# Projection products with 512 columns in one instruction instead of two halves of 256

## The chip, the cores and the metric

The kernel runs on one core of a Trainium2 chip, alone. The metric is the device time of one execution in microseconds (us); the lower the better. Five engines of the core work beside each other, each through its own list of instructions: TensorE (PE in the profile, its weight loads apart as PEld), VectorE (DVE), ScalarE (ACT), GpSimd (POOL) and SyncE (SP), which here issues the transfers.

## The reference, cut to what matters

Attention in chunks of 64 tokens is followed by two feed-forward layers over the 4,608 tokens; all arrays are float32.

```python
scores = scale * np.matmul(q_c, k_c.transpose(0, 1, 2, 4, 3))      # 8 x 8 heads, 9 chunks of 64, depth 64
attn = np.exp(scores - np.max(scores, axis=-1, keepdims=True))
attn = attn / (np.sum(attn, axis=-1, keepdims=True) + 1e-09)
out = np.matmul(attn, v_c)
...
h = np.maximum(np.maximum(x @ w1, x @ w2), x @ w3)                 # (4608, 512) @ (512, 768), three times
x = h @ w_out                                                      # (4608, 768) @ (768, 512)
...
h = np.maximum(x @ w_in, 0.0)                                      # (4608, 512) @ (512, 2048)
return (h * h @ w_out).astype(np.float32)                          # (4608, 2048) @ (2048, 512)
```

## The kernel before

Tokens are worked on in 9 blocks of 512 (`b`). Every float32 operand of a large product is kept as a sum of two float32r tiles, a high and a low part (names that end in h and l), and a product is made of three: high by high, high by low, low by high.

**The first half of the program** (to about 704 us) does the attention and the first feed-forward layer. `proj` is one projection product: for a slice `f` of 128 of the 768 columns and one of the three weights `w` (0 to 2), it adds 4 depth slices by 3 pairs into one bank `p` of PSUM (128 x 512). There are 9 x 6 x 3 = 162 of them, and two `p` banks that alternate. What comes out is taken by ScalarE for w = 0 (line 383) and by VectorE for w = 1 and 2 (lines 386 and 390), so product n + 2 can begin when product n has been taken. `g2` is the first output product: for each of the 6 slices `f` it adds 3 pairs into each of 4 `y` banks; there are 54 x 4 such groups. Both go through `mm_k` and `halves`, line 355. Before the change `halves` gives each pair as two instructions of 256 columns (HC = 256), which follow each other with the same weights. Three of the projection products at the very start are made in two parts of 256 columns each (`parts=2`), so that `dst` has only 256 columns there and `halves` has nothing to cut.

The blocks 2 to 8 run the loop `for f: for w: p1(b, f, w)`, with one step of the attention (scores S, transposes T, outputs X) after w = 0 as long as there is attention to do, and the output product of the slice before after w = 1. In the last block there is no attention left. In the first 125 us the input arrives, weights are split by ScalarE, VectorE and GpSimd, and a hand-made order of attention and products runs. A few bfloat16 products of zeros (`heat`, line 568, 512 columns each) stand in gaps there.

**The second half** (the products `z` of line 449 and `o` of line 500) uses Strassen's seven products on 256-column operands. The change doesn't touch it.

The weights of w = 1 lie in tiles of `shifted`, whose parts begin 64 bytes (SH = 16 floats) later than they would without it; those of w = 0 and 2 and of the output product lie in plain tiles.

Up to the projections of blocks 0 and 1 the order of the instructions is as written; from there on a scheduler sets it from the order in the code.

Of the kernel before, what the change touches and what calls it, by code (L numbers as in the profile page):

```python
# [23 lines left out]
HC = 256  # L24
# [17 lines left out]
def kernel(ctx: ExitStack, tc, qkv, w123, w_out, w_in2, w_out2, out):  # L42


    nc = tc.nc
# [298 lines left out]
    def mm_k(dst, wpair, xpair, k, first, last):  # L344

        (wh, wl), (xh, xl) = wpair, xpair
        halves(dst, ((wh, xh), (wh, xl), (wl, xh)), first, last)

    def halves(dst, pairs, first, last):


        for j, (lhs, rhs) in enumerate(pairs):
            for i in range(dst.shape[-1] // HC):
                c = slice(i * HC, i * HC + HC)
                nc.tensor.matmul(  # L355
                    dst[:, c], lhsT=lhs, rhs=rhs[:, c], start=first and i == 0 and j == 0,
                    stop=last and j == len(pairs) - 1, skip_group_check=True,
                )

    def proj(wpair, xpair, name, parts=1):  # L360

# [214 lines left out]
    first = tc.manual_schedule()  # L576
# [32 lines left out]
    def chunk(w, halves):  # L609
        if len(w) == 2:  # L610
            return g2(*w)
        if w not in parts:
            parts[w] = proj(W123[w[1:]], x_t[w[0]], f"p{w[2]}", 2 if halves else 1)
        p = next(parts[w])
        if p is not None:
            ends.append(p1_end(*w, p))
# [119 lines left out]
    last = None  # L736
    more = iter(())
    for b in range(NB):
        for g in range(NG):
# [20 lines left out]
            last = (a, (b, g))  # L760
# [79 lines left out]
```

## Time and profile before

| what | value |
|---|---|
| runs, device time | 1402.1, 1402.88 and 1403.73 us, median 1402.88 |
| profiled execution, first to last instruction | 1401.4 us |
| TensorE products, busy | 1376.2 us (98%) |
| TensorE weight loads, busy | 1358.6 us (97%) |
| VectorE, ScalarE, GpSimd, busy | 963.6, 492.4 and 237.4 us |

The page gives the profiled execution by its span alone. An instruction of TensorE is counted as busy from its start to its modelled end, so that neighbours in the pipeline overlap; the pace is read from the distance of two starts, not from the mean duration.

### The profile page before, as it was taken

To read this page: it belongs to the slowest core of one execution; us is meant where nothing else is said; L and a number is where in the kernel's file an instruction comes from. 1 tells how busy PE (TensorE), PEld (TensorE's weight loads), DVE (VectorE), ACT (ScalarE), POOL (GpSimd) and SP (SyncE) were. 2 spreads that over 40 slices of the span, in tenths; PEclk is the share of its full clock that TensorE was granted. 3 is DMA by queue.
4 is the path that set the end of the run, shared out by engine and by line. 5 is a ranking of instruction groups with operands and counts; after the bars stand their busy time and mean duration, and the time that the engine had idled before them with its cause. 6 is when DMAs were issued, how large, how long until landed. Compare 5 with 4: busy or idle time off the path is not lost.

```text
span 1401.4 us, 32734 instructions
## 1 busy us (share of the span) xinstructions
PE 1376.2 (98%) x13719; PEld 1358.6 (97%) x13719; DVE 963.6 (69%) x1525; ACT 492.4 (35%) x848; POOL 237.4 (17%) x204
## 2 busy tenths in 40 slices
PE   8889999999999999999999999999999999999998
PEld 5889999999999999999999999999999999999998
DVE  7998657677758577723266666666677888877774
ACT  3433233332323332411133333333334444444442
POOL 3654213332514323300000000000000000000000
PEclk9999999999999999999999999999999999999999
DMA  9332244653735554626643343343498444334341
GB/s 281 100 103 91 95 133 136 219 174 106 263 129 174 196 189 137 248 70 212 195 146 134 136 149 139 136 149 138 178 350 307 144 143 137 128 129 150 123 140 41
DMA packets 101236, 222.33 MB, mean 159 GB/s; under 512 B 11232, under 2 KB 20448, under 8 KB 101088
## 3 DMA queue, kind: packets, MB, share of 16 engines
q1 hardware_dynamic: 101088, 220.25, 46.1%
q8 instruction: 107, 1.75, 0.5%
q14 instruction: 41, 0.34, 0.1%
HBM read 134.22 MB, written 85.98 MB: 157 GB/s over the span
## 4 chain that ended last, share of the span: by engine, by line
PE 85%; DVE 1%; issue 0%; POOLq 0%; POOL 0%; ACT 0%; DVEq 0%; ACTq 0%
PE o L500 25%; PE z L449 25%; PE p L355 24%; PE y L355 9%; PE X L330 1%; PE S L278 1%; PE T L307 1%; DVE pl L207 0%; DVE u L472 0%; POOL u L472 0%; POOLq L836 0%; DVE mx L285 0%; DVE sm L295 0%; DVE e L288 0%; DVE h L390 0%
## 5 line engine op out<-in xcount | busy, mean ns | idle before, releaser
L449 PE MATMUL z<-yxh,wih 128*128 128x256 f32 x560 | 154.9, 277 | 0.0
L449 PE MATMUL z<-yxh,wil 128*128 128x256 f32 x560 | 154.7, 276 | 0.0
L449 PE MATMUL z<-yxl,wih 128*128 128x256 f32 x560 | 154.7, 276 | 0.0
L500 PE MATMUL o<-wo2h,gl 128*128 128x256 f32 x504 | 140.7, 279 | 0.0
L472 POOL TENSOR_TENSOR u<-u,s 128x512 f32<-128x512 f32 x9 | 11.7, 1296 | 761.5 <-DVE u L472 761.5
L500 PE MATMUL o<-wo2h,gh 128*128 128x256 f32 x504 | 140.4, 279 | 0.0
L500 PE MATMUL o<-wo2l,gh 128*128 128x256 f32 x504 | 140.2, 278 | 0.0
L500 PE MATMUL o<-wo2h,gxl 128*128 128x256 f32 x504 | 140.1, 278 | 0.0
L500 PE MATMUL o<-wo2h,gxh 128*128 128x256 f32 x504 | 139.9, 278 | 0.0
L500 PE MATMUL o<-wo2l,gxh 128*128 128x256 f32 x504 | 139.9, 278 | 0.0
L472 DVE TENSOR_TENSOR c<-z,s 128x512 f32<-128x512 f32 x108 | 74.3, 688 | 89.2 <-PE z L449 84.7
L449 PE MATMUL z<-yh,wih 128*128 128x256 f32 x448 | 124.2, 277 | 0.0
L449 PE MATMUL z<-yh,wil 128*128 128x256 f32 x448 | 124.1, 277 | 0.0
L449 PE MATMUL z<-yl,wih 128*128 128x256 f32 x448 | 124.1, 277 | 0.0
L392 ACT CAST hh<-h 128x512 fp32r<-128x512 f32 x54 | 33.5, 621 | 220.4 <-DVE h L390 209.4
L390 DVE TENSOR_TENSOR h<-p,m 128x512 f32<-128x512 f32 x54 | 37.1, 687 | 107.0 <-PE p L355 107.0
L457 ACT COPY s<-z 128x512 f32<-128x512 f32 x108 | 63.3, 586 | 133.7 <-PE z L449 132.4
L449 PEld LDWEIGHTS z<-yxh,wih 128*128 128x128 f32 x560 | 105.2, 188 | 0.2 <-DVE c L472 0.2
L449 PEld LDWEIGHTS z<-yxh,wil 128*128 128x128 f32 x560 | 105.1, 188 | 0.0
L449 PEld LDWEIGHTS z<-yxl,wih 128*128 128x128 f32 x560 | 105.1, 188 | 0.0
L500 PEld LDWEIGHTS o<-wo2l,gh 128*128 128x128 f32 x504 | 94.9, 188 | 0.0
L500 PEld LDWEIGHTS o<-wo2h,gl 128*128 128x128 f32 x504 | 94.7, 188 | 0.0
(196 smaller groups left out, 4160.1 us busy)
## 6 DMA issues: line engine op xcount, KB each, us to landing
gd<-g SPq DMA_DIRECT2D x144, 256.0 KB, 2.0
gr<-gd SPq DMA_DIRECT2D x72, 512.0 KB, 4.2
qk<-in_qkv SPq DMA_DIRECT2D x28, 512.0 KB, 4.3
raw<-in_w_out SPq DMA_DIRECT2D x22, 512.0 KB, 5.0
raw<-in_w SPq DMA_DIRECT2D x18, 512.0 KB, 3.5
v<-in_qkv SPq DMA_DIRECT2D x72, 128.0 KB, 5.9
yd<-ys SPq DMA_DIRECT2D x36, 256.0 KB, 2.8
yr<-yd SPq DMA_DIRECT2D x18, 512.0 KB, 5.0
```

The costliest lines, as they stand in the source:

```text
L278: nc.tensor.matmul(s_t[t][o:o + D, h ^ t % 2, :], lhsT=q[r, h, :], rhs=k[r, h, :], start=True, stop=True,)
L307: nc.tensor.transpose(tp[:, p * P:(p + 1) * P], e[:, 2 * p:2 * p + 2, :].rearrange("p h k -> p (h k)"), ident)
L330: nc.tensor.matmul(xps_t[t][j * D:j * D + D, p, c * D:c * D + D], lhsT=v[o:o + D, c, p, :], rhs=et[o:o + D, p, q:q + D], start=True, stop= ...
L355: nc.tensor.matmul(dst[:, c], lhsT=lhs, rhs=rhs[:, c], start=first and i == 0 and j == 0, stop=last and j == len(pairs) - 1, skip_group_ch ...
L390: nc.vector.tensor_tensor(out=h, in0=p, in1=st[b], op=ALU.max)
L392: nc.scalar.copy(hh, h)
L449: nc.tensor.matmul(dst[:, a * HC:a * HC + HC], lhsT=l[:, a, w], rhs=r[:, k, :], start=first and a + k + j == 0, stop=j == 2, skip_group_ch ...
L457: nc.scalar.copy(t, bank[tag])
L472: (eng or nc.vector).tensor_tensor(out=t, in0=x, in1=y, op=ALU.add)
L500: nc.tensor.matmul(bank[i][:, m * HC:m * HC + HC], lhsT=l[:, a, t], rhs=r[:, a, :], start=g + m + a + j == 0, stop=g == NG - 1 and j == 2, ...
```

## The change

The loop over halves goes. A pair is now one instruction over all the columns of `dst`: 512, and 256 in the three products made in parts.

```diff
         for j, (lhs, rhs) in enumerate(pairs):
-            for i in range(dst.shape[-1] // HC):
-                c = slice(i * HC, i * HC + HC)
-                nc.tensor.matmul(
-                    dst[:, c], lhsT=lhs, rhs=rhs[:, c], start=first and i == 0 and j == 0,
-                    stop=last and j == len(pairs) - 1, skip_group_check=True,
-                )
+            nc.tensor.matmul(
+                dst, lhsT=lhs, rhs=rhs, start=first and j == 0,
+                stop=last and j == len(pairs) - 1, skip_group_check=True,
+            )
```

The list of TensorE shows it, here at the end of a projection product, an attention output and the first group of an output product. Before:

```order
L355 MATMUL p_888<-xl_262,w_1h 128x256 x2
L355 MATMUL p_888<-xh_261,w_1l 128x256 x2
L330 MATMUL X<-et,v 64x64 x16
L355 MATMUL y_942<-hh,wo0h 128x256 x2
L355 MATMUL y_942<-hl,wo0h 128x256 x2
L355 MATMUL y_942<-hh,wo0l 128x256 x2
```

With the change, at the same place (the line is 353 there):

```order
L353 MATMUL p_852<-xl_262,w_1h 128x512
L353 MATMUL p_852<-xh_261,w_1l 128x512
L330 MATMUL X<-et,v 64x64 x16
L353 MATMUL y_894<-hh,wo0h 128x512
L353 MATMUL y_894<-hl,wo0h 128x512
L353 MATMUL y_894<-hh,wo0l 128x512
```

Each row with x2 has become one of 512 columns, and the order of the rows on TensorE is the same in the whole program. On VectorE the scheduler moves a few instructions past each other, once a step that takes a product out (m, line 386). Before:

```order
L288 TENSOR_TENSOR e<-S,mx 128x512 x2
L207 TENSOR_TENSOR pl<-t_8084,ph 128x512
L295 TENSOR_REDUCE sm<-e 128x8 x2
L298 TENSOR_SCALAR sm<-sm 128x8
L386 TENSOR_TENSOR m_8167<-p_8142,s_8074 128x512
```

With the change:

```order
L288 TENSOR_TENSOR e<-S,mx 128x512 x2
L384 TENSOR_TENSOR m_6127<-p_6114,s_6046 128x512
L295 TENSOR_REDUCE sm<-e 128x8 x2
L298 TENSOR_SCALAR sm<-sm 128x8
L207 TENSOR_TENSOR pl<-t_6056,ph 128x512
```

The step m now stands ahead of the sums of the softmax, and the low part pl behind them. Some ten rows move in this way on VectorE, one on ScalarE, three on SP, and none on GpSimd.

## Rows read from the trace of the kernel before

**Rows 1.** The page: busy time of each engine, and the chain that ended last.

```profile
span 1401.4 us, 32734 instructions
PE 1376.2 (98%) x13719; PEld 1358.6 (97%) x13719; DVE 963.6 (69%) x1525; ACT 492.4 (35%) x848; POOL 237.4 (17%) x204
PE o L500 25%; PE z L449 25%; PE p L355 24%; PE y L355 9%; PE X L330 1%; PE S L278 1%; PE T L307 1%; DVE pl L207 0%; DVE u L472 0%; POOL u L472 0%; POOLq L836 0%; DVE mx L285 0%; DVE sm L295 0%; DVE e L288 0%; DVE h L390 0%
```

**Rows 2.** Stretches of the first half, all engines: busy us (instructions), granted clock, DMA.

```profile
0.00:125.00 125.00, 106.88 (x1172) 96.08 (x1173) 111.13 (x167) 46.28 (x78) 64.92 (x52) 0.96 0.50 152
125.00:200.00 75.00, 73.94 (x908) 72.33 (x907) 46.18 (x77) 21.68 (x37) 20.26 (x16) 1.00 0.33 111
200.00:620.00 420.00, 419.37 (x4894) 414.71 (x4894) 280.87 (x465) 135.02 (x238) 128.54 (x118) 1.00 0.51 172
620.00:704.00 84.00, 83.99 (x733) 83.80 (x732) 26.17 (x41) 16.61 (x29) 0.00 (x0) 1.00 0.52 170
```

**Rows 3.** The same stretches, line 355 alone: PE and PEld busy us.

```profile
0.00:125.00 125.00, 76.05 (x589) 73.27 (x590) 0.96 0.50 152
125.00:200.00 75.00, 67.35 (x572) 65.61 (x571) 1.00 0.33 111
200.00:620.00 420.00, 388.32 (x3326) 381.53 (x3326) 1.00 0.51 172
620.00:704.00 84.00, 81.02 (x704) 80.57 (x702) 1.00 0.52 170
```

**Rows 4.** The chain that ended last, from 212 us: start, us, instructions.

```profile
212.43 2.98 PE p L355 x24
215.41 2.72 PE y L355 x24
218.13 5.44 PE p L355 x48
```

**Rows 5.** Timeline of TensorE and its weight loads at 800 us: start, us.

```profile
799.93 0.28 PE L449 MATMUL z<-yxh,wih 128*128 128x256 f32 x1
799.93 0.19 PEld L449 LDWEIGHTS z<-yxl,wih 128*128 128x128 f32 x1
800.04 0.28 PE L449 MATMUL z<-yxl,wih 128*128 128x256 f32 x1
800.05 0.19 PEld L449 LDWEIGHTS z<-yxh,wil 128*128 128x128 f32 x1
```

**Rows 6.** Timeline of TensorE from 11.58 us: bfloat16 products of 512 columns, transposes.

```profile
11.58 2.33 PE L568 MATMUL warm<-zero 128*128 128x512 bf16 x10
13.75 0.60 PE L307 MATMUL T<-ident,e 128*128 128x128 f32 x4
14.19 0.81 PE L568 MATMUL warm<-zero 128*128 128x512 bf16 x3
```

**Rows 7.** Lines 568 and 307: duration ns min/median/max, first and last start.

```profile
L568 PEld LDWEIGHTS <-zero x39: 95/98/151, 1.2 to 21.7; 128*128 128x128 bf16 x39
L568 PE MATMUL warm<-zero x39: 379/379/634, 1.2 to 21.9; 128*128 128x512 bf16 x39
L307 PE MATMUL T<-ident,e x144: 270/272/383, 13.8 to 600.1; 128*128 128x128 f32 x144
```

**Rows 8.** Timeline of TensorE at 31.7 us, in a stretch at half clock.

```profile
31.70 0.41 PE L355 MATMUL p<-xh,w_0h 128*128 128x256 f32 x1
31.91 0.41 PE L355 MATMUL p<-xl,w_0h 128*128 128x256 f32 x1
32.12 0.41 PE L355 MATMUL p<-xh,w_0l 128*128 128x256 f32 x1
```

**Rows 9.** Weight loads that waited: us in total, times, longest.

```profile
PEld p L355 <- ACT s L383: 7.0, 4, 3.5
PEld p L355 <- DVE m L386: 2.2, 2, 1.3
PEld p L355 <- DVE h L390: 1.2, 1, 1.2
```

**Rows 10.** VectorE from 200 to 620 us, line 386: busy us, mean ns, idle before.

```profile
L386 DVE TENSOR_TENSOR m<-p,s 128x512 f32<-128x512 f32 x35 | 24.0, 685 | 28.6 <-PE p L355 28.6
```

**Rows 11.** Timeline of TensorE in the last block, end of w = 0, then w = 1.

```profile
622.96 0.39 PE L355 MATMUL p<-xl,w_5h 128*128 128x256 f32 x2
623.18 0.39 PE L355 MATMUL p<-xh,w_5l 128*128 128x256 f32 x2
623.41 0.39 PE L355 MATMUL p<-xh,w_5h 128*128 128x256 f32 x2
...
626.01 0.40 PE L355 MATMUL p<-xh,w_5l 128*128 128x256 f32 x2
626.25 0.39 PE L355 MATMUL y<-hh,wo4h 128*128 128x256 f32 x2
```

## The prediction

> **What bounds the kernel now.** I read the page first. TensorE's products are busy for 98% of the span and its weight loads for 97%, VectorE for 69%, and the chain that ended last is TensorE nearly throughout; the two groups that the change touches, p and y of line 355, hold 24% and 9% of it [rows 1]. Then I cut the first half into stretches, to see where that holds. From 200 to 620 us TensorE is busy for 419.37 of 420 us and from 620 to 704 us for 83.99 of 84, at full clock, while VectorE has 280.87 of 420 and 26.17 of 84. Only before 125 us is TensorE not the bound: 106.88 of 125 us, with VectorE at 111.13 and the clock at 0.96 [rows 2]. So after 125 us a nanosecond that TensorE saves per instruction is a nanosecond of the end, and before it only in part.
>
> Since busy times overlap, the pace has to come from starts. The chain shows 24 products of y in 2.72 us and 48 of p in 5.44 us [rows 4]: 113.3 ns for each instruction of 256 columns, 226.7 ns for a pair of halves. At half clock two starts lie 0.21 us apart (31.70, 31.91, 32.12) [rows 8]. If that is pure streaming, 256 columns cost 213 ns there, and at full clock half of it, 106.7 ns. So at full clock 6.7 ns of the 113.3 are something else.
>
> What that is, the weight loads tell. Each load starts when the product before it starts (799.93 and 799.93, 800.04 and 800.05), and the product that uses it starts 0.11 us after the load (800.04) [rows 5]. A chain is closed: product starts, load starts, 110 ns later the next product starts. That the load alone is that long is seen in the transposes, which stream only 128 columns and still take (0.60 - 0.272) / 3 = 109 ns from start to start [rows 6, 7]. So I read the 256-column pace as that of the 4-byte weight load (109 ns, and some 4 ns of start-up), which just covers the streaming of 107 ns.
>
> **The change part by part.** *What goes.* By the code, line 355 issues 162 x 24 + 54 x 24 = 5,184 instructions, of which 72, in the three products made in parts, stay as they are. The other 5,112 become 2,556, each with one weight load instead of two. The rows have 589 of the old ones before 125 us, with the 72 among them [rows 3], so (589 - 72) / 2 = 258 pairs there, and 2,298 after it.
>
> *What one instruction of 512 columns costs.* The trace has no float32r product that wide, so it is bounded from both sides. Below, streaming alone at full clock: 2 x 106.7 = 213.3 ns. The nearest row is the bfloat16 product of zeros with 512 columns: (2.33 - 0.379) / 9 = 217 ns and (0.81 - 0.379) / 2 = 216 ns from start to start [rows 6, 7]. It differs in having a weight load of 98 ns and half the bytes to read. The upper bounds are the pair as it is, 226.7 ns, if what limits goes with the bytes, and the pace of a disturbed product (below), 236.7 ns. I take 216 ns: it is the row with the same count of columns, and a load of 110 ns, started with the product before, lies wholly beside 213 ns of streaming. The saving is 226.7 - 216 = 10.7 ns per pair.
>
> *What it sums to.* After 125 us: 2,298 x 10.7 ns = 24.6 us. Before: 258 x 10.7 ns = 2.8 us, of which I take half, 1.4 us, between nothing (VectorE and the weights set the pace) and all of it. Together 26.0 us, so the span goes from 1401.4 to 1375.4 us. The median of the runs stood 1.5 us above the profiled span; 1376.9, so **1377 us**.
>
> *What could be late next.* A projection product shrinks from 2.72 to 12 x 0.216 = 2.59 us, and the one after next needs its bank. Taking it out is one instruction of 0.685 us on VectorE [rows 10], or about as much on ScalarE, and the three rows of waits for it hold 10.4 us in seven waits [rows 9]; from 200 us on, TensorE's idle time of all kinds is 0.63 us up to 620 us [rows 2]. Losing 0.13 us of 2.72 I cost at nothing; it is covered by the next product, and if that cover were gone, each late step would cost at most its own 0.7 us. VectorE's share from 200 to 620 us goes from 280.87 / 420 = 67% to about 70%. The few rows that the scheduler moves on VectorE, ScalarE and SP shift work by an instruction or two; one of them takes a product out earlier. I cost them at nothing for the same cover. Nothing changes on SP's queue but two neighbours at a time, and the second half starts with the same loads in flight.
>
> *The clock.* The 0.96 before 125 us is 10 us at half clock, some 5 us of time [rows 2]. When TensorE is through sooner there, its idle stretches grow; one shorter or longer slow stretch is worth a few us either way. I put nothing into the sum, and 4 to 5 us into the range.
>
> **The rivals.**
>
> *B: the 6.7 ns belong to each instruction, not to the load.* Then 512 columns cost 213.3 + 6.7 = 220 ns and a pair saves 6.7 ns: 2,298 x 6.7 = 15.4 us and 0.9 us before, together 16.3, which gives 1386.6 us. For it speaks that I cannot see what the 4 ns of start-up are; against it, that the load's start and the product's are chained to 110 ns, and that the bfloat16 row of 512 has an overhead of only 3 ns.
>
> *C: reading the moving operand is the limit.* A float32r column has twice the bytes of the bfloat16 one. At the pace of now, 256 x 4 bytes come in 113.3 ns, 9.0 bytes per ns in a partition; if that is all there is, 512 columns take 226.7 ns as before, and the time stays at 1402.9 us. For it: nothing in the trace shows a faster rate. Against it: in the same 113.3 ns 512 bytes of weights are read too, and with the change half as many.
> [...]
>
> *D, the other sign: weight load and moving operand get in each other's way in every instruction.* In the last block, the product with w = 1 (weights 64 bytes further on) is slower than its neighbours: from 623.41 to 626.25 us, 24 instructions in 2.84 us, 118.3 ns each, against 0.22 to 0.23 us a pair just before [rows 11]. The same instructions on the same engine; only the place of the weights differs. So a load beside the stream can cost 5 ns in 113. Now load and product keep step, one load to each 256 columns. With 512 columns the load ends in the middle of the stream, and the step between the two is no longer fixed. If every 256 columns then ran as in the disturbed product, 512 would take 236.7 ns, 10.0 ns more than a pair now: 2,556 x 10.0 = 25.6 us, 1428.5 us. It decides from the point where a 512-column instruction costs over 226.7 ns, 10.7 more than I take. Against it: half as many loads, and one disturbance of 5 ns in each would make 221 ns, still faster than now.
> [...]
>
> **How the numbers follow.** Chances: 216 ns (my forecast) 0.48; B 0.20; C 0.12; D 0.18; anything else that ends slower, such as late banks, 0.02. The forecast's own range is 1371 (all 2.8 us before 125 us, and the slow clock there gone: 24.6 + 2.8 + 5 = 32.4 us off) to 1382 (nothing before 125 us, and 4 us of clock lost). The range over the cases reaches from there to C with 4 us of clock on top, 1407: A, B and C hold 0.80, and D is left out. Runs of this kernel agree within about 0.1%, so a change of 0.2%, 2.8 us, is about what can be told from none. Faster by more than that are my forecast and B, 0.68; within it C, 0.12; slower D and the rest, 0.20.
>
> **What would show it.** In the profile after, line 353 has 2,556 products of 128x512 and 72 of 128x256, and as many loads. Right: in a chain row, 12 products of y in 2.59 us where 24 stood in 2.72; each load still starts with the product before it, and then idles for about 100 ns; weight-load busy time falls well below the products' in 200 to 620 us; that stretch's work takes about 18 us less; z and o keep 113 ns. 220 or 227 ns from start to start means B or C; anything above 227, with products of w = 0 and w = 2 above it too, means D. Wrong in another way: the pace is 216 but TensorE now stands idle after 200 us before p, waiting for lines 381, 384 or 388, or the span before 125 us grows with more time at half clock.

## The result, and the profile after

| | before | after |
|---|---|---|
| median of the runs, us | 1402.83 (1402.1 to 1403.73, 4 runs) | 1413.87 (1411.54 to 1414.44, 4 runs) |
| profiled execution: its time, span, us | see above, span 1401.4 | 1411.54, span 1409.8 |
| ratio of the runs | | 1.0067, interval 1.0053 to 1.0081 |

The kernel became 0.67% slower (0.53 to 0.81; the medians differ by 11.0 us, 0.79%). I had forecast 1377 us, so the sign was wrong, and the time lies 7 us above the top of the range. The profiled execution is the quickest of the four of after: spans in the profile differ by 8.4 us, and what is read from spans below is to be set beside that.

The page of the kernel after, the busy times of its engines and the chain that ended last:

```profile
PE 1385.3 (98%) x11163; PEld 1246.0 (88%) x11163; DVE 961.3 (68%) x1525; ACT 492.8 (35%) x848; POOL 236.4 (17%) x204
PE p L353 28%; PE o L498 25%; PE z L447 24%; PE y L353 10%; PE X L330 1%; PE S L278 1%; DVE a L105 1%; PE T L307 1%; DVE a L107 1%; DVE a L110 1%; DMA raw<-in_w 1%; DMA v<-in_qkv 1%; DMA k<-in_qkv 1%; DVE hl L392 1%; DVE s L116 0%
```

2,556 products and as many loads have gone, the loads' busy time fell from 97% to 88% of the span, and TensorE stayed busy for 98% of it. The groups that were changed grew: p from 24% to 28% and y from 9% to 10% of the chain [rows 1]. Line 353 here is line 355 of before.

Stretches of the kernel after, all engines (busy us and instructions of PE, PEld, DVE, ACT, POOL, then the granted clock):

```profile
0.00:125.00 125.00, 106.17 (x918) 82.80 (x919) 109.74 (x167) 46.10 (x78) 64.66 (x52) 0.97 0.51 150
200.00:620.00 420.00, 420.00 (x3200) 337.28 (x3199) 277.85 (x462) 134.44 (x237) 127.74 (x118) 1.00 0.51 169
...
200.00:706.60 506.60, 506.60 (x3572) 406.93 (x3571) 299.91 (x495) 146.56 (x257) 127.74 (x118) 1.00 0.51 169
706.60:1056.00 349.40, 349.40 (x3048) 348.46 (x3047) 233.36 (x360) 124.61 (x214) 0.00 (x0) 1.00 0.46 163
```

The kernel before, from 200 us to the end of its first half, and the same piece of the second half:

```profile
200.00:697.70 497.70, 497.07 (x5573) 492.41 (x5573) 300.94 (x495) 146.22 (x257) 128.54 (x118) 1.00 0.52 173
697.70:1047.00 349.30, 349.29 (x3060) 348.89 (x3059) 233.29 (x360) 124.52 (x214) 0.00 (x0) 1.00 0.46 164
```

This places the loss. The second half is the same to 0.1 us (349.3 and 349.4). The 37th projection product, the first of block 2, begins at 199.37 us before and at 199.38 after, so what stands ahead of it neither won nor lost. What grew is the work from 200 us to the end of the first half, from 497.7 to 506.6 us: 8.9 us. VectorE, ScalarE and GpSimd have the same instructions in it (495, 257, 118), and TensorE's last 0.63 us of idle time are gone. So TensorE itself takes longer for the same columns.

The same stretches of the kernel after, line 353 alone:

```profile
200.00:620.00 420.00, 388.96 (x1632) 302.87 (x1631) 1.00 0.51 169
620.00:704.00 84.00, 84.00 (x361) 67.57 (x361) 1.00 0.52 169
```

The chain that ended last in the kernel after (start, us), the place of [rows 4]:

```profile
212.67 3.00 PE p L353 x12
215.67 2.80 PE y L353 x12
218.47 5.60 PE p L353 x24
```

Twelve products of y in 2.80 us are 233.3 ns each; [rows 4] had a pair of halves in 226.7. Single starts of y lie 233 or 234 ns apart throughout, those of p 232.9 on average.

TensorE and its weight loads in the kernel after, the place of [rows 5] (start, us):

```profile
302.25 0.39 PE L353 MATMUL y<-hl,wo1h 128*128 128x512 f32 x1
302.26 0.19 PEld L353 LDWEIGHTS y<-hh,wo1l 128*128 128x128 f32 x1
302.49 0.39 PE L353 MATMUL y<-hh,wo1l 128*128 128x512 f32 x1
```

The load still starts with the product before it (302.26 and 302.25). Products of 128 and 192 columns, whose pace the load sets, come every 111.7 ns (experiment 1), so here some 120 ns are left over. The load is no longer near being late, and the product comes at 233 ns all the same.

The kernel after in a stretch at the 1.2 GHz level, beside [rows 8]:

```profile
86.55 0.63 PE L353 MATMUL p<-xl,w_1h 128*128 128x512 f32 x1
86.97 0.63 PE L353 MATMUL p<-xh,w_1l 128*128 128x512 f32 x1
```

Here 512 columns take 0.42 to 0.43 us, twice the 0.21 of 256: at this level nothing is lost and nothing won. Whatever costs the time is there at the 2.4 GHz level alone.

**The sum.** After 200 us there are 1,632 + 361 = 1,993 products of 512 columns, 233.3 - 226.7 = 6.67 ns dearer each: 13.3 us. Against that, the slow stretches with w = 1 [rows 11] are gone, about 2.8 us (experiment 6 measured 2.5), and the idle 0.63 us. That makes 9.9 us; 8.9 were measured, and 1 us is not accounted for.

### The profile page after: what moved, and what is told of

The parts are those of the page before. It is cut to its first block, busy times and chain, and to the rows that moved or that the text cites. A ratio compares the mean times of both kernels' runs of the same rounds, so it can differ in the third digit from the quotient of the medians.

```text
span 1409.8 us, 27683 instructions
## 1 busy us (share of the span) xinstructions
PE 1385.3 (98%) x11163; PEld 1246.0 (88%) x11163; DVE 961.3 (68%) x1525; ACT 492.8 (35%) x848; POOL 236.4 (17%) x204
## 4 chain that ended last, share of the span: by engine, by line
PE 91%; DVE 5%; DMA 2%; issue 1%; ACT 1%; POOL 0%; SPq 0%; POOLq 0%; DVEq 0%; ACTq 0%
PE p L353 28%; PE o L498 25%; PE z L447 24%; PE y L353 10%; PE X L330 1%; PE S L278 1%; DVE a L105 1%; PE T L307 1%; DVE a L107 1%; DVE a L110 1%; DMA raw<-in_w 1%; DMA v<-in_qkv 1%; DMA k<-in_qkv 1%; DVE hl L392 1%; DVE s L116 0%
```

## The experiments

Two questions stood after the result. Is 226.7 ns a floor that no split can get under, and what sets it: the weight load, the stream of columns, the accumulation? And why does the whole instruction not reach it? Below, a half is an instruction of 256 columns, a whole one of 512, and the 64-byte place of an operand is where it begins, counted in steps of 64 bytes: two operands lie at the same place when they differ by an even number of such steps.

**1. The disputed cost by itself.** A kernel that runs only sequences of 48 products on TensorE, one varied thing at a time. The weights stand 64 bytes on in their tile (`SH`), the operand does not.

```python
    seq("c128x", 128)
    seq("c192x", 192)
    seq("c256x", 256)
...
    seq("c512x", 512)
    seq("same256x", 256, wo=0)
    seq("same512x", 512, wo=0)
    seq("fresh512x", 512, each=True)
...
    seq("bf512x", 512, bf=True)
...
    seq("w32c512x", 512, cols=32)
    seq("w64c256x", 256, cols=64)
...
```

> This kernel leaves out the whole computation and runs only sequences of 48 float32r products on TensorE, each sequence with its own tile, so that the distance of two starts can be read for each width and each form. Three theories for the 233 ns between two 512-column starts of the changed kernel (227 ns for two of 256 before, 216 ns for bfloat16). Theory W (the width itself: reading a float32r operand of 512 columns can't keep up over so long a run, whatever the weights do): the distance over 2 columns per 0.83 ns grows faster than the width, 113 ns at 256, some 170 to 175 at 384, 233 at 512; weights of 64 or 32 columns at 512 stay at 233; no accumulation stays at 233; bfloat16 stays at 216. Theory L (the weight load disturbs the stream): 512 with 64-column weights falls about half way to 216, 225 or less, and with 32-column weights further, under 222; the place of the weights changes 512 by 5 ns or more. Theory A (adding into a full bank costs): 512 without accumulation falls to about 216, and bfloat16 that accumulates rises to 233.

The timeline of that kernel (start, us, of a sequence; a pace is the distance to the next start, divided by 48, or read from single starts inside):

```profile
31.19 5.47 PE L73 MATMUL c128x<-mv,wt 128*128 128x128 f32 x48
36.50 5.55 PE L73 MATMUL c192x<-mv,wt 128*128 128x192 f32 x48
41.89 5.84 PE L73 MATMUL c256x<-mv,wt 128*128 128x256 f32 x48
47.56 7.20 PE L73 MATMUL c320x<-mv,wt 128*128 128x320 f32 x48
...
72.78 11.37 PE L73 MATMUL c512x<-mv,wt 128*128 128x512 f32 x48
83.98 5.90 PE L73 MATMUL same256x<-mv,wt 128*128 128x256 f32 x48
89.72 11.07 PE L73 MATMUL same512x<-mv,wt 128*128 128x512 f32 x48
100.63 11.36 PE L73 MATMUL fresh512x<-mv,wt 128*128 128x512 f32 x48
...
117.49 10.53 PE L73 MATMUL bf512x<-mb,wb 128*128 128x512 bf16 x47
...
144.27 11.28 PE L73 MATMUL w32c512x<-mv,wt 128*32 128x512 f32 x48
155.38 5.88 PE L73 MATMUL w64c256x<-mv,wt 128*64 128x256 f32 x48
```

128 and 192 columns both come every 111.7 ns: that is the pace of the weight load, and 256 columns stand above it. With 512 columns the price is 233.3 ns, and it stays when each product starts an accumulation of its own (233.3) and when only 32 columns of weights are loaded (231.7); 256 columns with half the weights take 119.0, with all of them 117.8. So neither the length of the load nor the accumulation sets the pace. bfloat16 with 512 columns is at 215.8 ns, the price that I had taken. What does change the float32r price is where the two operands stand: with both at the same 64-byte place, 512 columns take 226.7 ns ((100.63 - 89.72) / 48 = 227) and 256 take 120.0 instead of 117.8. A change of 5 ns or more with the place of the weights was a sign of theory L; it came, 6.6 ns, while L's other sign, a shorter load that helps, did not.

**2. The order of the halves.** The kernel before with its two loops exchanged, still 256 columns.

```diff
-        for j, (lhs, rhs) in enumerate(pairs):
-            for i in range(dst.shape[-1] // HC):
+        for i in range(dst.shape[-1] // HC):
+            for j, (lhs, rhs) in enumerate(pairs):
```

> The kernel before, still 256 columns per instruction, but for each depth slice the three pairs are done for the first half and then for the second, so that no two instructions that follow each other have the same weights. Theory W (width): 113.3 ns per instruction as before, 1402.9 us within 0.2%. A rival by which the pace of before comes from loading the same weights twice: the pace rises towards 117 ns per instruction and the time towards 1410 us or more.

1417.89 us against 1403.62, ratio 1.0102 (1.0087 to 1.0117): slower than the whole instruction. The chain of that kernel:

```profile
642.11 8.49 PE p L355 x72
650.61 2.83 PE y L355 x24
```

Both come at 117.9 ns an instruction (2.83 / 24), where [rows 4] has 113.3. Halving by itself is not what made the kernel before quick: two of these halves are dearer than a whole. It came out as the rival had it, by which the same weights twice in a row give the pace. Experiments 5 and 9 speak against that as a rule: there the exchanged order also runs at 113.3 ns (at C), and the order of the kernel before also at 117.8 (at A).

**3. One part alone.** Only the output product y with 512 columns, p in halves as before; `whole` is the loop of the kernel after.

```diff
-            mm_k(yacc[b][d], (wh[:, a, c], wl[:, a, c]), hp, f, f == 0, f == NF1 - 1)
+            (hh, hl), l, r = hp, wh[:, a, c], wl[:, a, c]
+            whole(yacc[b][d], ((l, hh), (l, hl), (r, hh)), f == 0, f == NF1 - 1)
```

> The kernel before, but the 648 pairs of the output product alone are 512 columns wide; the projections stay in halves. Theory W: 648 x 6.7 ns = 4.3 us more, 1407 us, with 233 ns between starts of y. A rival by which the loss sits in the projections (their banks are freed too late, or the scheduler's other order on VectorE and SP costs it): within 1 us of 1402.9 us.

1406.24 us against 1403.62, ratio 1.0019 (1.0008 to 1.003). Its chain:

```profile
628.75 2.80 PE y L351 x12
631.55 8.28 PE p L362 x72
```

y costs 233.3 ns in this piece and p what it did (115.0, against 114.9 in the last block of the kernel before). 648 products at 6.67 ns would be 4.3 us; 2.6 were measured, with an interval of 1.1 to 4.2. So the loss belongs to the instructions that were widened, each where it stands.

**4. After, without the 64-byte offset of w = 1.** It is the one place where [rows 11] had shown that the weights' place counts.

```diff
-            hi, lo = [shifted(name + n).rearrange("p (a c) -> p a c", a=2)[:, :, SH:] for n in "hl"]
+            hi, lo = [halved(shifted(name + n)[:, 0:512]) for n in "hl"]
```

> The changed kernel, but the weights of w = 1 lie without the 64-byte offset of their parts. Theory W: 512-column products cost 233 ns wherever the weights lie, so the time stays within 1 us of the changed kernel's 1413.9 us. Theory L: the products of w = 1 change by 5 ns or more per instruction, 648 x 5 ns = 3 us or more, one way or the other.

1412.68 us, ratio 1.0066 (1.0051 to 1.0081), the same as the kernel after. p is at 232.9 ns and y at 233.0: with whole instructions this offset changes nothing. In the last block of the kernel after, the products with w = 1 come every 232.7 to 233.6 ns, like the others.

**5. The place of the two operands.** Sequences of 48 again, with tiles of their own for weights and operand, in four places: A operand 64 bytes on, as in the kernel; B neither; C weights 64 bytes on; D both.

```python
    runs = [(w, 0, x, c, 256) for w, x in three for c in (0, 256)]
    outer = [(w, 0, x, c, 256) for c in (0, 256) for w, x in three]
    whole = [(w, 0, x, 0, 512) for w, x in three]
    one = [(w, 0, x, 0, 256) for w, x in three]
    two = [(WH, 0, XH, c, 256) for c in (0, 256)]
    full = [(WH, 0, XH, 0, 512)]
...
    for tag, wo, mo in (("A", 0, SH), ("B", 0, 0), ("C", SH, 0), ("D", SH, SH)):
```

> This kernel leaves out the whole computation and runs sequences of 48 float32r products in the orders of the kernels: runs (each of three weight and operand pairs for the first 256 columns and then for the second, as before the change), outer (three pairs for the first 256 columns, then three for the second), whole (three pairs of 512 columns, as with the change), one (three pairs, always the first 256 columns), two (one pair, the halves in turn), full (one pair, 512 columns). Each stands four times, by the 64-byte place of weights and moving operand: A moving operand 64 bytes on, as in most of the kernel's products; B neither; C the weights 64 bytes on; D both. Theory W in the form that the first sequences leave (reading a float32r operand has a floor of about 113.3 ns per 256 columns, 226.7 per 512, and order and place decide how much is lost above it): in A, runs 113.3, outer near 118, whole near 233, so that the order alone makes the difference of the second kernel; no sequence of 512 columns under 226.7 and none of 256 under 113. A rival by which the program around it sets the loss (other engines that read the same memory): all of A at 113.3 and 226.7.

The timeline of that kernel, halves (two) and wholes (full) at A, B and C, and the halves of A once more at the end (16 products, whose single starts lie 117 to 119 ns apart):

```profile
58.45 5.60 PE L65 MATMUL twoAx<-xh,wh 128*128 128x256 f32 x48
63.89 11.15 PE L65 MATMUL fullAx<-xh,wh 128*128 128x512 f32 x48
...
103.93 5.92 PE L65 MATMUL twoBx<-xh,wh 128*128 128x256 f32 x48
109.69 11.07 PE L65 MATMUL fullBx<-xh,wh 128*128 128x512 f32 x48
...
149.03 5.60 PE L65 MATMUL twoCx<-xh,wh 128*128 128x256 f32 x48
154.47 11.36 PE L65 MATMUL fullCx<-xh,wh 128*128 128x512 f32 x48
...
212.23 2.10 PE L65 MATMUL last<-xh,wh 128*128 128x256 f32 x16
```

The same 48 halves take (63.89 - 58.45) / 48 = 113.3 ns at A, 120.0 at B and 113.3 at C; a whole takes 228.9, 226.7 and 233.3. D gives what B does. Nowhere is a whole below 226.7 or a half below 113.3: that is the floor, and halves and wholes reach it at different places. My guess for the order fell: at A the runs of the kernel before came at 117.8 ns like the outer order, and the very pairs that ran at 113.3 came at 117.8 at the end. So place is not all of it. Nor did the wholes at A come near 233, as I had expected. By the sizes of the tiles A is the place of w = 0, w = 2 and y in the kernel, where a whole takes some 233 ns, and here it takes 228.9; with its offset w = 1 stands as at D, and takes 233 there too, and here 226.7. So these sequences give the floor, but not the pace of the wholes in the kernel. What the kernel adds, transfers and other engines among it, was not tested by itself.

**6. Before, without the offset of w = 1** (the edit of 4 on the kernel before).

> The kernel before, but the weights of w = 1 lie without the 64-byte offset of their parts, so that like those of w = 0 and 2 they differ from the moving operand by an odd number of 64-byte lines. Theory that the place decides: the slow stretches of w = 1 (10 gaps of 5.5 ns in 35 products and 23 in 7) go to 113.3 ns, 2.8 us less, 1400.5 us if before is 1403.3. Rival by which w = 1 is slow for its place in the loop, behind the attention step: no change within 0.5 us.

1401.23 us against 1402.85 (11 and 15 runs), ratio 0.9982 (0.9973 to 0.9991): quicker than both kernels, by little. 2.8 us were expected, and 2.5 (1.3 to 3.8) were measured. Its chain:

```profile
650.17 8.16 PE p L355 x72
```

All of p, w = 1 with it, is now at 113.3 ns.

**7. After, with operand and weights of the projections at one place.** The edit of 4, and the tiles of x 64 bytes on; by experiment 5 wholes should then come to 226.7.

```diff
-                x_t[b] = (
-                    ap.tile([P, KD, TB], F32R, tag="xh", name=f"xh{b}"),
-                    ap.tile([P, KD, TB], F32R, tag="xl", name=f"xl{b}"),
+                x_t[b] = tuple(
+                    ap.tile([P, KD * TB + 2 * SH], F32R, tag=n, name=f"{n}{b}")[:, SH:SH + KD * TB]
+                    .rearrange("p (k t) -> p k t", k=KD) for n in ("xh", "xl")
                 )
```

> The changed kernel (512 columns), but the tokens' operands of the projections begin 64 bytes further on and the weights of w = 1 don't, so that moving operand and weights of all projections lie at the same 64-byte place, which in the sequences of the second bench gave 226.7 ns for 512 columns. Theory that the place relative to each other decides what 512 columns cost: p goes from 233 to 226.7 ns, 1,908 x 6.7 = 12.7 us less than the changed kernel without the offset (1412.7 us), 1400 us; y stays at 233 ns. A rival by which the program around it (transfers, other engines) costs the 6.7 ns: p stays at 231 to 233 ns, 1412 us.

1408.93 us, ratio 1.0041 (1.0027 to 1.0055). Its timeline late in the first half, where products with w = 2, w = 0 and w = 1 begin, and the output product behind them:

```profile
655.56 0.39 PE L353 MATMUL p<-xh,w_1h 128*128 128x512 f32 x1
...
658.32 0.39 PE L353 MATMUL p<-xh,w_2h 128*128 128x512 f32 x1
...
661.04 0.39 PE L353 MATMUL p<-xh,w_2h 128*128 128x512 f32 x1
...
663.82 0.40 PE L353 MATMUL y<-hh,wo1h 128*128 128x512 f32 x1
```

The 36 products take 8.26 us, 229.4 ns each; on average over the run p takes 230.8, against 232.9 in experiment 4: the right direction, a third of the size. Of 12.7 us expected from the projections some 4 came. The three weights differ: w = 2 takes 230 ns here (2.76 us for 12), w = 0 stands on the floor of 226.7 (2.72 us), with all the program around it, and w = 1 takes 231 to 232 (2.78 us). All three are at the same place by the edit, so place alone does not give the pace. Products that no edit was meant to touch moved as well: z went from 114.1 to 115.2 ns (3.5 us lost), o from 115.8 to 114.7 (3.1 us won). The edit makes the x tiles 128 bytes longer, and their buffers are used for operands of z and o later on, so those stand elsewhere in memory too; whether that moved them was not tested.

**8. The halves at that place** (the two edits of 7 on the kernel before). If the place favours wholes, it should hurt halves.

> The kernel before (halves), with the same two moves of place as the run with 512 columns: moving operand and weights of all projections at the same 64-byte place. Theory that the place decides, and the other way round for halves: p goes from 113.3 to between 118 and 120 ns per instruction, 3,888 x 4.5 to 6.7 = 17 to 26 us more than 1401.2 us, so 1418 to 1427 us. The rival by which halves are good in themselves: 1401 us.

1422.55 us, ratio 1.0126 (1.0109 to 1.0143). Its chain:

```profile
645.71 8.57 PE p L355 x72
```

119.0 ns in this piece, 119.1 on average. The same two edits took 4 to 6 us off the whole instructions (1.0067 to 1.0041 by the ratios, 11.0 to 5.4 us above before by the medians) and put 19 us on the halves: place and width act together, which no rule about width alone gives. Not all of the 19 us is p: it takes 4.8 ns more than in the kernel before, 14.6 us after 200 us, and y, whose instructions were not edited, went from 113.4 to 116.7 ns, another 3.3 us.

**9. The same sequences, entered in different ways.** Experiment 5 had one sequence at two paces. Either the order of the products decides, or a pace, once there, stays.

```python
        seq(f"one{tag}ax", one, wo, mo, 16)
        seq(f"outer{tag}ax", outer, wo, mo)
        seq(f"runs{tag}ax", runs, wo, mo)
        seq(f"kick{tag}ax", slow, wo, mo, 4)
        seq(f"runs{tag}bx", runs, wo, mo)
        seq(f"outer{tag}bx", outer, wo, mo)
        seq(f"one{tag}bx", one, wo, mo, 16)
...
```

> This kernel leaves out the whole computation and repeats the sequences of the second bench with the operand and the weights at different 64-byte places, each order several times, entered from different sequences before it (kick: products of 128 columns, which the loads set the pace of). Theory S (such a sequence has two steady paces, and the one that it is in when it begins persists): runs and outer both show 113.3 ns behind a sequence that runs at 113.3, and 117.8 behind one that runs at 117.8 or behind a kick, whatever their order. Rival O (the order itself sets the pace): each name shows one pace only, runs 113.3 and outer 117.8, or each 117.8.

The timeline of that kernel at place C: the first and the last row of one sequence of 48 ahead of a kick of 16 products with 128 columns, and of the same sequence behind it:

```profile
108.23 0.40 PE L65 MATMUL runsCax<-xh,wh 128*128 128x256 f32 x2
...
113.64 0.40 PE L65 MATMUL runsCax<-xh,wl 128*128 128x256 f32 x2
113.88 1.90 PE L65 MATMUL kickCax<-xh,wh 128*128 128x128 f32 x16
116.13 0.39 PE L65 MATMUL runsCbx<-xh,wl 128*128 128x256 f32 x2
...
120.89 0.39 PE L65 MATMUL runsCbx<-xh,wl 128*128 128x256 f32 x2
```

Ahead of the kick 46 steps take 5.41 us, 117.6 ns each; behind it, once settled, 42 steps take 4.76 us, 113.3 each, and the two sequences that follow stay at 113.3. At A all of them, behind the kick too, stay at 117.8. So halves have two steady paces in one place, with the same order, and in this kernel a sequence of halves takes over the pace of the halves ahead of it, unless a kick at C stands between. That the pace behind a kick would be the slow one was wrong. Two things do not fit into this: at A in experiment 5 the pace went from 117.8 to 113.3 behind a sequence of wholes, and here, at A too, it stayed at 117.8 behind one; and exchanging the loops in experiment 2 moved p and y of the whole program to 117.9.

**10 and 11. Using that.** In the second output product o of the kernel of 6, of four slices the first two run at 118 ns and the last two at 113.3, in every block. The first pair of slice 1 (10), or all three (11), cut into products of 128 columns might reset the pace.

The line of 10 that decides which product is cut:

```diff
...
+                    parts = 2 if g == 0 and i == 1 and m + a == 0 and j == 0 else 1
...
```

> The kernel before with the weights of w = 1 not offset, and in the second half of the program, in each of the 9 blocks, the first pair of the product o1 of the first slice (it follows o2, whose operands lie at the same 64-byte place) is cut into two instructions of 128 columns, which the weight load sets the pace of. Theory S (two steady paces, and what comes before decides): the products of the first two slices of a block, 117.8 ns per instruction now, change to 113.3 as in the third bench behind such instructions with the weights 64 bytes on: 9 x 155 x 4.4 ns = 6.2 us less and 9 x 0.1 us more, 5.3 us under 1401.2 us, 1396 us. Rival: the pace belongs to the operands of these slices, 117.8 ns stay and the time rises by 1 us.

> As the run before, but all three of the first pairs are cut, six instructions of 128 columns in place of three of 256. Theory S: 113.3 ns behind them, 6.2 us less and 9 x 0.3 us more, 3.4 us under 1401.2 us, 1398 us; it also holds where a single cut pair is too short to change the pace. Rival: 117.8 ns stay, the time rises by 3 us.

1402.19 us, ratio 0.9988 (0.9979 to 0.9997), and 1403.5 us, 0.9999 (0.999 to 1.0008), against 1403.58. In both, slices 0 and 1 stay at 117.8 to 118.0 ns, as the rival had it. Beside the 0.9982 of experiment 6 the cuts cost some 1 and 2 us, the first not clear of noise; the rival had 1 and 3. The cut did not reset the pace, and what sets it is not found by this.

**12. Is it the reading?** If the operand's bytes are the limit, their reach should count, not the columns. Both operands at one place, 48 products each; `every(x, k, n)` takes every k-th column.

```python
    seq("next256x", W, XH[:, 0:256])
    seq("next512x", W, XH[:, 0:512])
    seq("every2c256x", W, every(XH, 2, 256))
    seq("every2c512x", W, every(XH, 2, 512))
    seq("every4c256x", W, every(XH, 4, 256))
...
    seq("same512x", W, XH[:, 0:1].to_broadcast([P, 512]))
    seq("bfnext512x", wb, mb[:, 0:512])
    seq("bfevery2c512x", wb, every(mb, 2, 512))
```

> This kernel leaves out the whole computation and runs sequences of 48 products on TensorE: float32r columns that follow each other, every second and every fourth column of a longer row, and one column read over and over; bfloat16 columns that follow each other and every second one. Theory W in the form of a limit of reading (float32r columns arrive more slowly than TensorE could take them at full clock because of how many 64-byte lines they lie in): every second column needs twice the lines and goes to clearly over 260 ns at 512 columns, one column over and over to under 220 ns, bfloat16 at every second column (as many lines as float32r columns that follow each other) from 216 to 227 ns or more. Rival M (the float32r form of the product has its own pace, whatever is read): 512 float32r columns cost 226 to 234 ns in each form, and bfloat16 216 ns in both.

The timeline of that kernel:

```profile
31.50 5.92 PE L68 MATMUL next256x<-xh,wh 128*128 128x256 f32 x48
37.25 11.07 PE L68 MATMUL next512x<-xh,wh 128*128 128x512 f32 x48
48.16 11.20 PE L68 MATMUL every2c256x<-xh,wh 128*128 128x256 f32 x48
59.19 21.93 PE L68 MATMUL every2c512x<-xh,wh 128*128 128x512 f32 x48
80.94 11.38 PE L68 MATMUL every4c256x<-xh,wh 128*128 128x256 f32 x48
...
103.13 10.66 PE L68 MATMUL same512x<-xh,wh 128*128 128x512 f32 x48
113.63 10.53 PE L68 MATMUL bfnext512x<-mb,wb 128*128 128x512 bf16 x48
124.00 11.00 PE L68 MATMUL bfevery2c512x<-mb,wb 128*128 128x512 bf16 x48
```

512 neighbouring columns take 226.7 ns, every second one 453.3, and one column over and over 218.7. 256 columns taken over the same 2,048 bytes take 230 ns, and 512 of bfloat16 over the same 2,048 bytes 225.8, where 512 neighbours of bfloat16, 1,024 bytes, have 215.8. Up to every second column the time goes with the bytes that are reached over, about 9 per ns in a partition. Every fourth column, though, costs hardly more than every second (233.3 and 230), over twice the bytes, so neither the reach nor the number of 64-byte lines is the limit without end. Rival M, a pace of the float32r form itself, has at most a small part: one column over and over is 2.9 ns above bfloat16, and 512 different ones are 10.9 above.

## Why the prediction was wrong

**The step that failed** is "So I read the 256-column pace as that of the 4-byte weight load". From it came the term of the sum that failed, 216 ns for 512 columns, and with it all of the gain; 233 ns were measured. The rows behind it were right, a load starts with the product before it and the transposes come every 109 ns, but they could not decide: two things of 107 to 113 ns each that start together look much the same whichever ends last. Experiment 1 parts them: load-paced products come every 111.7 ns, and at 512 columns a load of 32 columns leaves 231.7. Experiment 12 shows what was in its place, the mechanism of rival C: reading the moving operand, 226.7 ns for 512 different float32r columns at best, and 218.7 when one column is read over and over. The bfloat16 row that I took for the price reads half the bytes.

By the Trainium skill, "TensorE: Matmul & The Clock Gate", section "Back-to-back issue gap", a product by itself has a gap of N / 2.4 + 2.5 ns, by my estimate 215.8 at 512 columns; the section names no element type. The bfloat16 products of experiment 1, in a stream, come at the same 215.8; the float32r ones, at 226.7 to 233.3, do not.

The Trainium skill, "Advanced Engine Details and Errata", section "Memory Cachelines", asks for at least two hits on each 16-byte line if a read is to have its full rate. Every second float32r column hits a line twice, and 256 of them took 230 ns instead of 120; every fourth, with one hit, took hardly more (233.3). The runs here disagree with it.

**The argument against C fell.** I had held half as many weight bytes against it. With half the weights 256 columns took 119.0 ns and with all of them 117.8: fewer weight bytes did not make them faster.

**Why slower and not the same.** C alone would have given 1402.9 us. The floor is the same for a pair and for a whole, but the pairs of before stood on it (113.3 for a half), except those of w = 1, and the wholes stand 6.7 ns above it. That is 13.3 us after 200 us, less 2.8 for w = 1 and 0.6 of idle time. That the loss lies there is measured; why the wholes stand above the floor is not shown. The pace moves with the 64-byte places of both operands (experiments 5, 7, 8), and for halves a pace can last and be taken over (9). But at the places of the kernel the sequences gave 228.9 and 226.7 ns where the kernel has 233, and with all projections at one place w = 0 came to 226.7 and the others did not. What sets the pace stays open.

**Rival D** had the sign and the point from which it decides, 226.7 ns. Its mechanism, the load disturbing the stream, is not borne out: 32 columns of weights leave 231.7 of 233.3. What it took as its sign, that the place of the weights counts, is real. Its price, 236.7, was too high by 3.4 ns, and it did not count that w = 1 was already slow. I had named "above 227, with products of w = 0 and w = 2 above it too" as its sign; that came, and by itself did not tell a disturbing load from a pace that goes with place. Rival B's 220 ns was met nowhere.

**What held.** A nanosecond of TensorE after 125 us was a nanosecond of the end. Before it, the change was to bring between nothing and 2.8 us, and brought nothing. Banks, evictions and the rows that the scheduler moved cost nothing: TensorE idles for 0.00 us from 200 to 620 us. The clock before 125 us is 0.97 and was 0.96. z and o kept their pace, 114.0 and 115.8 ns on average; the 113 ns that I gave for both was z's alone.

## What to carry to other kernels

Take the price of a wider instruction from a row with the same element type: columns of 4 bytes and of 2 bytes have different limits at full clock, and a row with the same count of columns does not replace it. Where two things of equal length start together, the trace does not tell which of them is waited for; shorten one by itself before counting on the other. Before a product is merged or split, measure its start-to-start pace in its own place, in the kernel itself: here one edit of place was worth 4 to 6 us to the wide form and cost the narrow one 19, and undoing the 64-byte offset of w = 1 alone (0.9982) beat both kernels.

## What the runs showed of the hardware that was not expected

- At full clock, in sequences by themselves, 256 float32r columns have steady paces of 113.3, 117.8 and 120.0 ns, by where the operands stand and by what ran before, and 512 have 226.7, 228.9 and 233.3, by where the operands stand. The best place for halves (A or C) is not the best for wholes (B or D).
- A pace lasts: a sequence kept 117.8 ns over some 140 products, and 113.3 behind a kick of 16 short ones, in place C; in A the kick did nothing.
- At 1.2 GHz none of this is to be seen: 0.21 us for 256 columns and 0.42 to 0.43 for 512.
- Every second column costs as much time as all the float32r columns of the same reach: 230 ns for 256, in float32r; 225.8 for 512 in bfloat16, against 226.7 for the same 2,048 bytes of float32r columns side by side. Every fourth does not follow this: 256 take 233.3 ns.
